# Loops of the weighted sums on TensorE: ten rounds of six instead of six rounds of ten, and a loop in the last two units

## The chip, the core and the metric

The kernel runs on one core of a Trainium2 chip. A core has five engines with queues of their own: TensorE (PE, with the weight loads shown apart as PEld), VectorE (DVE), ScalarE (ACT), GpSimd (POOL) and SyncE (SP), which issues the transfers here; 16 DMA engines carry them out. The metric is the device time of one execution in microseconds, as the median over runs.

## What is computed

Eight sequences decode one token each. An attention with 32 query heads over 16 key and value heads reads the last 2048 positions of its caches (`W = 2048`); beside it stands a layer norm with a two-layer MLP; a sigmoid gate mixes the two results. All tensors are bf16. Cut to what matters:

```python
q = (x @ wq).reshape(B, 1, 32, 128)
scores = einsum(q, k_cache[:, :, Sk - W:]) * 128 ** -0.5
p = softmax(scores)
o = einsum(p, v_cache[:, :, Sk - W:])          # the weighted sum
a = o.reshape(B, 1, 4096) @ wo
h = gelu(layernorm(x) @ w1 + b1)
b = h @ w2 + b2
g = sigmoid((x * gate_w).sum(-1))
out = g * a + (1 - g) * b
```

The two caches make 134 MB of the 154 MB that are read from HBM.

## The kernel before

**Tiling.** The 128 pairs of sequence and key head and the 2048 positions are cut into 16 units (`NU`): 4 groups of two sequences (`NG`), and for each of them 4 parts of 512 positions (`NT`). A unit needs one K transfer and one V transfer of 4096 KB each. The buffer `RAW` has four slots of that size (`ND`); `take_slot` deals them out in the order 1, 2, 0, 3. The list `stream` (L587 to L594) sets the order of the transfers on SP's queue: K0, K1, V0, K2, V1, ..., K15, V14, V15, and then the first 24 parts of w2 ("M 0"), the two halves of wo ("W 0", "W 1") and the last 12 parts of w2 ("M 1", three transfers). A transfer waits until the last reader of its slot is done. For a slot that held V, the last reader is the unit's weighted sum (`slot_free[s] = [pv]`, L789). M 1 takes the slot of V14, and W 0 has a slot of its own.

**One unit.** VectorE transposes K in two halves (L718; in unit 15 in four quarters). TensorE writes a mask to PSUM (L685) and adds the scores to it (L732, the other three of four by the helper line L175). VectorE takes the maximum (L645), ScalarE the exponential with its sum (L646, L649). VectorE transposes the weights (L668) and ScalarE copies them in four parts into their places in `BD` (L674); in unit 15 eight smaller transposes of VectorE do that (L663, four for each half of the sum). Then TensorE forms the weighted sum of V: 64 matmuls of 128 x 256 (`NK // 2`), each with a weight load of its own, all added up in one place of PSUM.

**The weighted sum, where the change is.** `pair(e, n)` (L753 to L756) emits the n-th matmul of a unit with fixed addresses; it shows as L755. In units 0 to 13, `pv_loop` (L758) emits pairs 0 and 1, then a loop of `ROUNDS` = 6 rounds of `RND` = 10 matmuls whose addresses stand in two registers (`reg_matmul`, shown as L188; the registers are advanced at L770, and the branch of the loop is L767), and then pairs 62 and 63. In units 14 and 15 `pv_half` (L782) emits two halves of 32 fixed pairs; the first half of unit 15 can start when half of its weights are in place.

**Order on TensorE.** `_Plan.schedule` sorts all operations by their assumed costs; the lists `pe_hist` keep masks, scores and weighted sums in the order in which they are added: scores of unit t, weighted sum of unit t - 1, mask and scores of unit t + 1. ScalarE's copies (L674) of unit t wait for the weighted sum of unit t - 1 (L891 to L893), since both use `BD`. At the end the order on TensorE is: weighted sum of unit 13, mask and scores of unit 15, first half of unit 14, the group's maximum over its units (L695; L696 on VectorE waits for it), second half of unit 14, first half of unit 15, the group's sum (L703), second half of unit 15, two thirds of M 0's matmuls (L579), the selection matmuls (L819), the last third of M 0, the output projection with W 0 (L579), eight matmuls without a use for their result ("fill", L851 and L175), the projection with W 1, and the three pieces of M 1. Between the second half of unit 15 and the selection matmuls VectorE weights and adds up the four sums of the group (L794 to L808), and behind them it makes `oT` (L822), which both projections need. The last three operations are the copies out of PSUM (L900, L901) and the transfer of the output.

**What a plan's cost changes.** The costs given with an operation (8.8 for a loop, 3.65 for a half) only enter the sorting; the change leaves them as they are.

Of the kernel before, what the change touches and what calls it, by code (L numbers as in the profile page):

```python
# [38 lines left out]
class _Plan:  # L39
# [10 lines left out]
    def add(self, eng, fn, deps=(), name=None, cost=0.1, after=(), prio=0):  # L50
        op = _Op(eng, fn, deps, name, cost, after=after, prio=prio)
        op.idx = len(self.all)
        self.all.append(op)
        return op
# [116 lines left out]
ARENA_BASE = 16512  # L171
# [10 lines left out]
def reg_operand(reg, ap):  # L182
    return mybir.RegisterAccessPattern(ap=ap, dtype=BF, memsetref="arena_set", regref=reg.name, is_regloc_offset=False,
                                       reg_ap_offset=reg.name, const_ap_offset=0, const_sub_tensor_id=0)
# [10 lines left out]
def build_kernel(nc, A_x, A_k_cache, A_v_cache, A_wq, A_wo, B_x, B_w1, B_b1, B_w2, B_b2, gate_w, out):  # L195
    B, Sq, D = A_x.shape
    _, Hkv, Sk, Dh = A_k_cache.shape
# [10 lines left out]
    NK = W // (4 * NT)  # L208
    ND = 4
    SE = 4 * W  # L210
    DE = 2 * SE
# [13 lines left out]
    with ExitStack() as es:  # L225
# [74 lines left out]
        def aoffs(name):  # L300
            return R[name][0] // 2
# [4 lines left out]
        def view(name, parts=128):  # L306
            o, n, dt = R[name]
            a = arena[0:parts, o // 2: o // 2 + (n * (2 if dt == BF else 4)) // 2]
            if dt == F32:
                a = a.bitcast(F32)  # L310
            return a
# [33 lines left out]
        RAW = view("RAW")  # L345
# [6 lines left out]
        def slot(s):  # L352
            return RAW[:, s * DE:min((s + 1) * DE, ND * DE + WOR * D)]
# [8 lines left out]
        def col(i, parts=128):  # L362
# [17 lines left out]
        add, dma = P.add, P.dma  # L380
# [7 lines left out]
                   deps=[o_idf], name="r8", cost=0.2)  # L388
# [210 lines left out]
        qk_hist, pe_hist, dve_ops = [], [], {}  # L599
        qk_unit, qb_done = {}, {}  # L600
        exp_done, sp_done, pv_done, mx_done = {}, {}, {}, {}
# [11 lines left out]
        def load_item(which, nm, t):  # L613
            s = take_slot()
            g, xq = divmod(t, NT)
            k0 = S0 + 4 * NK * xq
            src = ck[which][32 * g:32 * g + 32, k0:k0 + 4 * NK, :].rearrange("i (x r) d -> i x (r d)", x=4)
            d = dma("sp", lambda e: e.dma_start(slot(s), src), "s%d" % s, 8 * W * Dh * 2, deps=slot_free[s], name="%s%d" % (nm, t), after=last_dma[-1:])
            last_dma.append(d)
            slot_free[s] = []  # L620
            return s, d
# [14 lines left out]
        def bd_home(t):  # L636
            return "KT" if t == NU - 1 else "BD"
# [108 lines left out]
        def v_item(t):  # L746
            s, d = load_item(1, "dv", t)
            g, x = divmod(t, NT)
            home = bd_home(t)
            obk, oc = (0, 0) if t == NU - 1 else (BK_OS + x // 2, 256 * (x % 2))  # L750
            dst = ps[:, obk, oc:oc + 256]

            def pair(e, n):  # L753
                q, ee = divmod(n, 2)
                return e.matmul(dst, bass.AP(arena, offset=aoffs(home) + 256 * q + ee, ap=[[AST, 128], [2, 128]]),  # L755
                                slot(s).rearrange("p (r k d) -> p r k d", r=2, d=128)[:, :, n, :], start=(n == 0), stop=(n == NK // 2 - 1), skip_group_check=True)  # L756

            def pv_loop(e):  # L758
                mm = None
                for n in range(2):  # L760
                    pair(e, n)
                if not regs:
                    regs.extend([e.alloc_register("r_p"), e.alloc_register("r_v")])
                rp, rv = regs
                e.reg_mov(rp, ARENA_BASE + 2 * (aoffs(home) + 256 + 254))
                e.reg_mov(rv, ARENA_BASE + 2 * (aoffs("RAW") + s * DE + 256))
                with e.Fori(0, ROUNDS) as _:  # L767
                    for i in range(RND):
                        reg_matmul(nc, e, dst, reg_operand(rp, [[AST, 128], [2, 128]]), reg_operand(rv, [[AST, 128], [DE // 2, 2], [1, 128]]))
                        e.reg_add(rp, rp, 2 if i % 2 == 0 else 510)  # L770
                        e.reg_add(rv, rv, 256)
                for n in range(2 + ROUNDS * RND, NK // 2):
                    mm = pair(e, n)
                return mm

            wait_x = [x_read[g - 1]] if g else [o_u]
            if t < NU - 2:
                pv = add("pe", pv_loop, deps=[d] + sp_done[t][0] + sp_done[t][1] + wait_x, name="pv%d" % t, cost=8.8, after=pe_hist[-1:])
                pe_hist.append(pv)
            else:  # L780
                for v in range(2):
                    def pv_half(e, v=v):  # L782
                        mm = None
                        for n in range(NK // 4 * v, NK // 4 * (v + 1)):
                            mm = pair(e, n)
                        return mm
                    pv = add("pe", pv_half, deps=[d] + sp_done[t][v] + wait_x, name="pv%d_%d" % (t, v), cost=3.65, after=pe_hist[-1:])
                    pe_hist.append(pv)
            slot_free[s] = [pv]  # L789
            src, w = ps[:, obk, oc:oc + 256], k(g, WT + x)  # L790
            if x == 0:
                fn = lambda e, src=src, w=w: e.tensor_scalar(out=X2, in0=src, scalar1=w, scalar2=None, op0=ALU.mult)
            else:
                fn = lambda e, src=src, w=w: e.scalar_tensor_tensor(out=X2, in0=src, scalar=w, in1=X2, op0=ALU.mult, op1=ALU.add)  # L794
            pend.append((fn, "x%d" % t, x))
            pv_of[t] = pv
            if x == NT - 1:
                last = None
                for fn, nm, xx in pend:
                    p = pv_of[t if t < NU - 1 and xx == 2 else NT * g + max(xx, 1)]  # L800
                    last = add("dve", fn, deps=[p, w_done[g], last, xl_done.get(g - 1)], name=nm, cost=0.5, prio=5 if g == NG - 1 else 0, after=dve_ops["sp", t] if xx < NT - 1 else [])
                del pend[:]
                x_read[g] = last
                x0 = add("dve", lambda e: e.tensor_scalar(out=X, in0=X2[:, 0:128], scalar1=maskq[:, 0:1], scalar2=None, op0=ALU.mult), deps=[last, o_maskq], name="xa%d" % g, cost=0.25, prio=6 if g == NG - 1 else 0)
                last = add("dve", lambda e: e.scalar_tensor_tensor(out=X, in0=X2[:, 128:256], scalar=maskq[:, 1:2], in1=X, op0=ALU.mult, op1=ALU.add), deps=[x0], name="xb%d" % g, cost=0.3, prio=6 if g == NG - 1 else 0)

                hi = add("dve", lambda e: e.tensor_copy(XS[:, 0, :], X), deps=[last, oT_done.get(g - 1)], name="xh%d" % g, cost=0.23, prio=6 if g == NG - 1 else 0)
                lo = add("dve", lambda e: e.tensor_tensor(out=XS[:, 1, :], in0=X, in1=XS[:, 0, :], op=ALU.subtract), deps=[hi], name="xl%d" % g, cost=0.3, prio=6 if g == NG - 1 else 0)  # L808

                xl_done[g] = lo  # L810

                def sel_x(e):
                    mm = None
                    for b in range(NB_):
                        for dq in range(4):
                            for v in range(2):
                                args = (ps[:, BK_S, 64 + 32 * b:64 + 32 * b + 32], seld[:, 4 * b + dq, :], XS[:, v, 32 * dq:32 * dq + 32])
                                st, sp = dq == 0 and v == 0, dq == 3 and v == 1
                                mm = e.matmul(*args, start=st, stop=sp, skip_group_check=True) if v == 0 else held_matmul(nc, e, *args, start=st, stop=sp, skip=True)  # L819
                    return mm  # L820
                sx = add("pe", sel_x, deps=[lo] + o_seld + [oT_done.get(g - 1)] + b6_r[-1:], name="sx%d" % g, cost=0.6, prio=3 if g == NG - 1 else 0)
                oT_done[g] = add("dve", lambda e: e.tensor_tensor(out=bass.AP(arena, offset=aoffs("oT") + NB_ * g, ap=[[AST, 128], [1, NB_], [8, WOP]]),  # L822
                                                                  in0=ps[:, BK_S, 64:128].rearrange("p (b j) -> p b j", b=2),
                                                                  in1=bass.AP(arena_f, offset=foffs("rg"), ap=[[AST // 2, 128], [1, NB_], [0, WOP]]), op=ALU.mult),
                                 deps=[sx, rg_done[g]], name="oT%d" % g, cost=0.45, prio=6 if g == NG - 1 else 0)
                b6_r.append(oT_done[g])

        pend, pv_of, xl_done = [], {}, {}
        regs = []
        ROUNDS, RND = 6, 10  # L830

        def wo_chunk(i):
            s = ND if i == 0 else take_slot()
# [123 lines left out]
```

## Time and profile before

The times of three runs are 364.46, 364.51 and 364.79 us: median 364.51. The profiled execution has a span of 363.0 us, from the first to the last instruction.

| | before |
|---|---|
| median of runs | 364.51 us |
| span of the profiled execution | 363.0 us |
| PE busy | 297.9 us (82%) |
| VectorE busy | 231.4 us (64%) |
| ScalarE busy | 168.6 us (46%) |
| HBM read | 154.29 MB, 425 GB/s over the span |
| looped matmuls (L188) | 840, 277 ns each |
| matmuls with fixed addresses (L755) | 184, 272 ns each |
| branches of the loops (L767) | 84 |

How to read it: matmuls are pipelined, and 277 ns is the way of one from its start to its end, while the next one starts much earlier; the pace is read from the starts in the timeline. "PE" rows are matmuls and "PEld" rows the weight loads ahead of them. A row of the timeline has the start in us, the length, the engine, the line and, in brackets, the idle time of the engine before it and what ended it; "issue" means that the engine waited for nothing that the profile shows. Branches and register instructions are not counted as busy. The page's 40 slices cover 9 us each.

### The profile page before, as it was taken

To read this page: it belongs to the slowest core of one execution; us is meant where nothing else is said; L and a number is where in the kernel's file an instruction comes from. 1 tells how busy PE (TensorE), PEld (TensorE's weight loads), DVE (VectorE), ACT (ScalarE), POOL (GpSimd) and SP (SyncE) were. 2 spreads that over 40 slices of the span, in tenths; PEclk is the share of its full clock that TensorE was granted. 3 is DMA by queue.
4 is the path that set the end of the run, shared out by engine and by line. 5 is a ranking of instruction groups with operands and counts; after the bars stand their busy time and mean duration, and the time that the engine had idled before them with its cause. 6 is when DMAs were issued, how large, how long until landed. Compare 5 with 4: busy or idle time off the path is not lost.

```text
span 363.0 us, 4821 instructions
## 1 busy us (share of the span) xinstructions
PE 297.9 (82%) x1954; PEld 125.3 (35%) x1423; DVE 231.4 (64%) x166; ACT 168.6 (46%) x130; POOL 22.9 (6%) x52
## 2 busy tenths in 40 slices
PE   0456366999999979998897979997989698999875
PEld 0111000434252615242433417150615152436742
DVE  0452989576666694929385768566675949295720
ACT  1022106656647463663637373838374554656000
POOL 9032030000010000000100000000000000003000
PEclk9976598999999998999999989999999999999999
DMA  8999999999999999999999999999999999999996
GB/s 347 436 437 406 455 412 455 412 455 412 450 415 451 415 451 413 441 426 441 426 441 426 435 430 437 430 437 428 437 430 437 430 435 430 437 430 433 415 430 257
DMA packets 6102, 154.45 MB, mean 426 GB/s; under 512 B 694, under 2 KB 840, under 8 KB 1228
## 3 DMA queue, kind: packets, MB, share of 16 engines
q1 hardware_dynamic: 6092, 154.30, 98.8%
q8 instruction: 8, 0.13, 0.1%
q14 instruction: 2, 0.02, 0.0%
HBM read 154.29 MB, written 0.01 MB: 425 GB/s over the span
## 4 chain that ended last, share of the span: by engine, by line
DMA 56%; DVE 27%; PE 14%; issue 1%; ACT 1%; SPq 0%; POOL 0%
DMA arena<-in_A_k_cache_dram 47%; DVE arena L718 21%; PE ps L175 6%; DMA arena<-in_B_w_dram 6%; DMA arena<-in_A_x_dram 3%; DVE arena L668 2%; PE ps L188 2%; PE ps L755 2%; PE ps L732 2%; DVE arena L645 1%; PE ps L501 0%; PE ps L579 0%; DVE arena L557 0%; DVE arena L521 0%; ACT arena L536 0%
## 5 line engine op out<-in xcount | busy, mean ns | idle before, releaser
L718 DVE STREAM_TRANSPOSE arena<-arena 128x4096 f32<-128x4096 f32 (+1 forms) x34 | 141.7, 4175 | 21.9 <-DMA arena<-in_A_k_cache_dram 21.9
L674 ACT ACTIVATE arena<-arena 32x2048 bf16<-32x2048 bf16 x60 | 114.5, 1908 | 71.4 <-DVE arena L668 42.9
L175 PE MATMUL ps<-arena 128*128 128x512 bf16 (+3 forms) x531 | 136.1, 402 | 0.0
L188 PE MATMUL ps<-arena 128*128 x840 | 109.5, 277 | 7.3 <-issue 1.2
L188 PEld LDWEIGHTS ps<-arena 128*128 x840 | 81.4, 97 | 34.3 <-issue 19.0
L732 PE MATMUL ps<-arena 128*128 128x512 bf16 x128 | 51.4, 401 | 27.6 <-DVE arena L718 26.1
L645 DVE TENSOR_REDUCE arena<-ps 128x1 f32<-128x2048 f32 x16 | 36.7, 2291 | 53.8 <-PE ps L175 53.8
L732 PEld LDWEIGHTS ps<-arena 128*128 128x128 bf16 x128 | 12.5, 98 | 131.7 <-issue 75.3
L649 ACT ACTIVATE arena<-ps,arena 128x2048 bf16<-128x2048 f32 x16 | 40.7, 2543 | 0.5
L646 ACT ACTIVATE arena<-arena 128x1 f32<-128x1 f32 x16 | 3.2, 203 | 63.5 <-DVE arena L645 63.5
L755 PE MATMUL ps<-arena 128*128 128x256 bf16 x184 | 25.3, 272 | 1.1 <-DVE arena L663 1.1
L755 PEld LDWEIGHTS ps<-arena 128*128 128x128 bf16 x184 | 16.9, 99 | 18.8 <-issue 14.6
L668 DVE STREAM_TRANSPOSE arena<-arena 128x1024 f32<-128x1024 f32 x15 | 18.1, 1205 | 2.9 <-ACT arena L649 2.9
L579 PE MATMUL ps<-arena 128*8 128x288 bf16 (+1 forms) x140 | 9.6, 286 | 4.0 <-DMA arena<-in_A_wo_dram 3.3
L739 POOL MEMSET arena<- 128x4096 f32 x1 | 3.5, 3511 | 148.2 <-PE ps L175 148.2
L685 PE MATMUL ps<-arena 128*128 128x512 bf16 x16 | 6.5, 407 | 6.5 <-ACT arena L649 5.2
L629 POOL COPY arena<-arena 32x64 bf16<-32x64 bf16 x16 | 3.7, 229 | 123.3 <-PE ps L175 122.4
L901 ACT ACTIVATE arena<-ps 8x288 bf16<-8x288 f32 x1 | 0.4, 402 | 19.5 <-PE ps L579 19.5
L422 DVE COPY arena<-arena 8x128 bf16<-8x128 bf16 x2 | 0.5, 228 | 13.9 <-DMA arena<-in_A_x_dram 13.9
L579 PEld LDWEIGHTS ps<-arena 128*8 128x8 bf16 (+1 forms) x140 | 5.8, 86 | 9.9 <-DMA arena<-in_A_wo_dram 3.3
L900 DVE CAST arena<-ps 8x288 bf16<-8x288 f32 x1 | 0.4, 446 | 12.3 <-PE ps L579 12.3
L557 DVE TENSOR_TENSOR arena<-arena 128x1152 f32<-128x1152 f32 x1 | 1.4, 1358 | 9.7 <-ACT arena L555 9.7
(106 smaller groups left out, 94.0 us busy)
## 6 DMA issues: line engine op xcount, KB each, us to landing
arena<-in_A_k_cache_dram SPq DMA_DIRECT2D x16, 4096.0 KB, 28.7
arena<-in_A_v_cache_dram SPq DMA_DIRECT2D x16, 4096.0 KB, 25.5
arena<-in_B_w_dram SPq DMA_DIRECT2D x1, 4608.0 KB, 22.0
arena<-in_A_wo_dram SPq DMA_DIRECT2D x2, 2304.0 KB, 23.8
arena<-in_A_wq_dram SPq DMA_DIRECT2D x1, 4096.0 KB, 12.6
arena<-in_B_w_dram SPq DMA_DIRECT2D x1, 3456.0 KB, 24.1
arena<-in_B_w_dram SPq DMA_DIRECT2D x1, 1152.0 KB, 22.3
arena<-in_B_w_dram SPq DMA_DIRECT2D x1, 576.0 KB, 23.0
```

The source lines that it names most:

```text
L175: return e.add_instruction(mybir.InstMatmult(name=nc.get_next_instruction_name(), engine=mybir.EngineType.PE, ins=[e.lower_ap(rhs), e.lowe ...
L188: return e.add_instruction(mybir.InstMatmult(name=nc.get_next_instruction_name(), engine=mybir.EngineType.PE, ins=[rhs, lhsT], outs=[e.low ...
L579: ins = e.matmul(ps[32 * j:32 * j + 8, BK_ACC, 0:JN], lhsT, rhs[:, JN * j:JN * j + JN], start=False, stop=True, skip_group_check=True, til ...
L629: return e.tensor_copy(dst, src)
L645: mx = add("dve", lambda e: e.tensor_reduce(out=k(g, MX + x), in_=scores, axis=AXL.X, op=ALU.max), deps=[qk_unit[t]], name="mx%d" % t, cos ...
L649: ex = add("act", lambda e: e.activation(out=bass.AP(arena, offset=aoffs("P"), ap=[[AST, 128], [64, 32], [1, 2], [2, 32]]), in_=ps[:, 0:4, ...
L668: pc = add("dve", lambda e: e.transpose(view("PC").bitcast(F32), view("P").bitcast(F32)), deps=[ex] + (sp_done[t - 1][0] if t else [o_acc0 ...
L674: return e.activation(out=bass.AP(arena, offset=32 * a * AST + aoffs(home) + 64 * a, ap=[[AST, 32], [256, 32], [1, 64]]), in_=bass.AP(aren ...
L685: mm = e.matmul(*args, start=True, stop=False, skip_group_check=True) if n == 0 else held_matmul(nc, e, *args, start=True, stop=False, ski ...
L718: return e.transpose(bass.AP(arena_f, offset=foffs(base) + 2048 * h0, ap=[[AST // 2, 128], [1, 2048 * nh]]), bass.AP(arena_f, offset=foffs ...
L732: mm = e.matmul(*args, start=False, stop=True, skip_group_check=True) if rc == 0 else held_matmul(nc, e, *args, stop=True, skip=True)
L755: return e.matmul(dst, bass.AP(arena, offset=aoffs(home) + 256 * q + ee, ap=[[AST, 128], [2, 128]]), slot(s).rearrange("p (r k d) -> p r k ...
```

## The change

`pv_loop` takes the range of its matmuls, the number of rounds and the matmuls in a round. Units 0 to 13 call it with 10 rounds of 6 (2 + 60 + 2 = 64 as before). The halves of units 14 and 15 call it too, with 7 rounds of 4 (2 + 28 + 2 = 32), so that the two registers are set and the loop is entered four more times.

```diff
-            def pv_loop(e):
+            def pv_loop(e, n0, n1, rounds, rnd):
                 mm = None
-                for n in range(2):
+                for n in range(n0, n0 + 2):
                     pair(e, n)
...
-                e.reg_mov(rp, ARENA_BASE + 2 * (aoffs(home) + 256 + 254))
-                e.reg_mov(rv, ARENA_BASE + 2 * (aoffs("RAW") + s * DE + 256))
-                with e.Fori(0, ROUNDS) as _:
-                    for i in range(RND):
+                e.reg_mov(rp, ARENA_BASE + 2 * (aoffs(home) + 128 * n0 + 256 + 254))
+                e.reg_mov(rv, ARENA_BASE + 2 * (aoffs("RAW") + s * DE + 128 * n0 + 256))
+                with e.Fori(0, rounds) as _:
+                    for i in range(rnd):
                         reg_matmul(nc, e, dst, reg_operand(rp, [[AST, 128], [2, 128]]), reg_operand(rv, [[AST, 128], [DE // 2, 2], [1, 128]]))
                         e.reg_add(rp, rp, 2 if i % 2 == 0 else 510)
                         e.reg_add(rv, rv, 256)
-                for n in range(2 + ROUNDS * RND, NK // 2):
+                for n in range(n0 + 2 + rounds * rnd, n1):
                     mm = pair(e, n)
                 return mm
...
-                pv = add("pe", pv_loop, deps=[d] + sp_done[t][0] + sp_done[t][1] + wait_x, name="pv%d" % t, cost=8.8, after=pe_hist[-1:])
+                pv = add("pe", lambda e: pv_loop(e, 0, NK // 2, 10, 6), deps=[d] + sp_done[t][0] + sp_done[t][1] + wait_x, name="pv%d" % t, cost=8.8, after=pe_hist[-1:])
...
-                    def pv_half(e, v=v):
-                        mm = None
-                        for n in range(NK // 4 * v, NK // 4 * (v + 1)):
-                            mm = pair(e, n)
-                        return mm
-                    pv = add("pe", pv_half, deps=[d] + sp_done[t][v] + wait_x, name="pv%d_%d" % (t, v), cost=3.65, after=pe_hist[-1:])
+                    pv = add("pe", lambda e, v=v: pv_loop(e, NK // 4 * v, NK // 4 * (v + 1), 7, 4), deps=[d] + sp_done[t][v] + wait_x, name="pv%d_%d" % (t, v), cost=3.65, after=pe_hist[-1:])
...
-        ROUNDS, RND = 6, 10
```

## The prediction

> **What bounds the kernel now.** I read the page first (busy time, the 40 slices, the DMA queues), then the chain of waits, then the timeline of the last 35 us and of single loops.
>
> ```profile
> span 363.0 us, 4821 instructions
> ...
> DMA  8999999999999999999999999999999999999996
> ...
> q1 hardware_dynamic: 6092, 154.30, 98.8%
> q8 instruction: 8, 0.13, 0.1%
> ```
>
> The 16 DMA engines are busy from the first slice to the last: 154.30 MB at 98.8%. The profiled execution has a span of 363.0 us, and the median of the runs is 364.51 us, so 1.5 us lie around the span; I carry that difference over unchanged. TensorE can only matter in two ways: it frees the buffers that the next transfers need, and it has work left when the last transfer has landed. The chain of waits (start, length, what) shows the second place:
>
> ```profile
> 312.51 0.22 PE ps L755 x2
> 312.73 1.14 PE ps L188 x10
> ...
> 319.80 1.33 PE ps L188 x10
> 321.13 0.36 PE ps L755 x2
> 321.49 0.22 PE ps L685
> ...
> 329.87 3.49 PE ps L755 x32
> 333.37 0.12 PE ps L695 x2
> 333.48 3.53 PE ps L755 x32
> ...
> 337.03 22.31 DMA arena<-in_B_w_dram
> ...
> 359.38 1.71 PE ps L579 x24
> ...
> 361.12 0.45 DVE arena L900
> ```
>
> Three things are to be seen. The weighted sum of unit 13 is a loop (L188) with two unrolled pairs (L755) on each side; from 312.51 to 321.49 it takes 8.98 us for 64 matmuls, 0.140 us each. The unrolled halves of unit 14 take 3.49 us for 32, 0.109 us each: looping is dearer. And the last weight transfer, issued at 337.03 when the second half of unit 14 frees its buffer, needs 22.31 us to land, because other transfers stand ahead of it in the queue; the kernel ends on that landing plus 24 small matmuls and the copy out.
>
> **What a round costs.** The timeline of the weight loads of unit 13 (start, length, engine, line; in brackets the idle time before):
>
> ```profile
> 316.91 1.15 PEld L188 LDWEIGHTS ps<-arena 128*128 x10 [0.33 <-issue]
> 318.35 1.15 PEld L188 LDWEIGHTS ps<-arena 128*128 x10 [0.30 <-issue]
> ```
>
> ```profile
> L767 PEldq COMPARE_BRANCH  x84: 69/201/235, 68.7 to 321.0; - x84
> ```
>
> A round of ten lasts 318.35 - 316.91 = 1.44 us. Inside it ten loads take 1.15 us; the last one itself is about 0.10, so the steps are (1.15 - 0.10) / 9 = 0.117 us. What is left, 1.44 - 1.17 = 0.27 to 0.28, is the round's end: a gap of 0.30 us in which nothing issues. The branch is in it: 84 branches are 14 units times 6 rounds, with a median of 201 ns, and the shortest (69 ns) are those that leave the loop. So I write a round of r matmuls as 0.117 r + b, with **b = 0.28 us** for each taken branch. The trace has rounds of one size only, so that b is the same for six and for four is an assumption. Its bounds: 0.31 (the 0.30 gap with the widest branch in place of the median, 0.235 - 0.201, less rounding) and, if a shorter body made the taken branch as cheap as the one that falls through, 0.28 - (0.201 - 0.069) = 0.15.
>
> [...]
>
> **The change part by part.** *Units 0 to 13, ten rounds of six.* The matmuls are the same 60; taken branches go from 5 to 9 per unit: 4 x 0.28 = +1.1 us of TensorE per unit. It is hidden by the transfers:
>
> ```profile
> DMA to landing us min/median/max: 18.8/25.5/37.3
> ...
> 60.00:134.00 74.00, 69.97 (x418) 28.82 (x299) 53.23 (x28) 45.50 (x33) 0.92 (x4) 1.00 1.00 432
> 134.00:298.00 164.00, 144.57 (x904) 61.97 (x652) 110.36 (x71) 89.11 (x64) 0.92 (x4) 0.98 1.00 432
> ```
>
> The first line is of the V transfers, which wait for a weighted sum to free a buffer; the other two are windows, with PE's busy time after the window's length. A 4 MB transfer takes 4.19 / 0.432 = 9.7 us, so even the V transfer with the shortest way (18.8 us) had 9 us of other transfers ahead of it. Between 60 and 134 us TensorE is nearly full (69.97 of 74) and falls behind by up to 1.1 us a unit, some 4 us over the four units there; that leaves 5 us of queue. Afterwards it has 19.4 us idle in 164 (8.5 units of 19.4 us), or 2.3 us a unit against 1.1, so it catches up before the last units. Without that cover the price would be up to 14 x 1.1 = 15 us; it would be gone only if b were about double. What is late next is unit 13, the last long loop: mask and scores of unit 15 follow it on TensorE, +1.1 us.
>
> *Units 14 and 15, four halves of seven rounds of four.* Per half: 28 looped matmuls at 0.117 in place of 0.109 (+0.2), six taken branches (6 x 0.28 = +1.68), the way out (the two pairs behind the loop above take 0.36 in place of 0.22, +0.14) and the two register loads at its start (below 0.1; I take 0.06): **+2.08 us** on 3.49. These stand one after the other on TensorE, and this is the view of what follows them:
>
> ```profile
> 321.59 7.70 ACT L674 ACTIVATE arena<-arena 32x2048 bf16<-32x2048 bf16 x4 [3.90 <-PE ps L755]
> ...
> 335.08 5.84 DVE L663 STREAM_TRANSPOSE arena<-arena 32x512 f32<-32x512 f32 x8 [1.41 <-ACT arena L649]
> ...
> 338.14 3.65 PE L755 MATMUL ps<-arena 128*128 128x256 bf16 x32 [1.14 <-DVE arena L663]
> ...
> 345.63 0.48 DVE L794 SCALAR_TENSOR_TENSOR arena<-ps,arena 128x256 f32<-128x256 f32 x1 [2.74 <-PE ps L755]
> 345.67 2.13 PE L579 MATMUL ps<-arena 128*8 128x288 bf16 x32
> ...
> 348.23 1.15 PE L579 MATMUL ps<-arena 128*8 128x288 bf16 x16
> 348.33 0.44 DVE L822 TENSOR_TENSOR arena<-ps,arena 128x64 bf16<-128x64 f32 x1 [0.92 <-PE ps L175]
> 351.23 2.13 PE L579 MATMUL ps<-arena 128*8 128x288 bf16 x32 [1.85 <-DMA arena<-in_A_wo_dram]
> 353.29 0.39 PE L851 MATMUL ps<-arena 128*128 128x512 bf16 x1
> 353.51 1.67 PE L175 MATMUL ps<-arena 128*128 128x512 bf16 x7
> 356.65 2.13 PE L579 MATMUL ps<-arena 128*8 128x288 bf16 x32 [1.46 <-DMA arena<-in_A_wo_dram]
> 359.38 1.70 PE L579 MATMUL ps<-arena 128*8 128x288 bf16 x24 [0.61 <-DMA arena<-in_B_w_dram]
> ```
>
> ScalarE's copies for unit 14 (L674) start on the end of unit 13's loop, so they are also 1.1 late, and the first half starts at 330.8. TensorE waits 1.14 us ahead of unit 15 for the transposes (L663); it now comes later than they do, so this wait is eaten. VectorE's minimum (L696) stands ahead of those transposes and waits for a matmul behind the first half: the transposes start about 2 us late, end by 343, and unit 15's halves start at 342.2 and 347.9; the first four of eight are done by 340, so nothing waits. The end of unit 15's sum, and with it L794, moves by
>
> 1.1 + 4 x 2.08 - 1.14 = **8.3 us**.
>
> The weight transfers issued at 337.03 go out at 342.2; of their 22.31 us about 4 are their own 1.7 MB, so 18 us of queue stand ahead and 5 us less do not show. That step costs nothing.
>
> Then the tail. L822, which makes the attention result, ends at 357.1 in place of 348.8; the 16 matmuls ahead of the first output projection end at 357.45, and the projection starts there, not at 351.23 (it waited for a landing, 1.85). It keeps 2.06 us to the filler; the eight filler matmuls take 8 x 0.213 = 1.71 (from 1.67 for seven); the second projection starts at 361.2 in place of 356.65. Its 32 matmuls take 1.90 at (2.13 - 0.29) / 31 = 0.0595 each, the 24 last ones 1.37 to the last start plus 0.29: 364.8 in place of 361.1. The tail had 4.6 us of slack, and **3.7 us** come through: 364.51 + 3.7 = **368.2 us**. In general: shift = 28 b + 0.46, end = 364.5 + (shift - 4.6) where that is positive.
>
> The code gets shorter; all of it is 8 packets and 0.13 MB by the page's row for q8, and a sixth less of that is below 0.1 us of DMA.
>
> **The rivals.** *No change* (the other side): the branch is cheaper in a short body, or TensorE's sequencer runs ahead. One mechanism decides: b. At 0.148 us the shift is 4.6 and everything fits in the waits for landings: 364.5 us. For it speaks that one loop did run at full pace:
>
> ```profile
> 218.82 6.71 PE L188 MATMUL ps<-arena 128*128 x60
> ```
>
> That is 0.109 each, branches hidden. Against it: there TensorE was busy with earlier matmuls for 2 us after the loop could issue; at the end the halves follow each other, and the only wait ahead of one (1.14) is eaten.
>
> *Dearer rounds.* In unit 12 the rounds took 301.77 - 300.03 = 1.74 us, 0.3 more than in unit 13:
>
> ```profile
> 300.03 1.38 PE L188 MATMUL ps<-arena 128*128 x10 [0.37 <-issue]
> 301.77 1.33 PE L188 MATMUL ps<-arena 128*128 x10 [0.36 <-issue]
> ```
>
> The trace does not say why this loop and not others. If it falls on one of the halves: 6 x 0.3 = +1.8, 370.0 us. [...]
>
> *Faster*: only by less instruction traffic, 0.1 us; I see no path to 0.2%.
>
> **How the numbers follow.** A measurement here tells about 0.2% (0.7 us) from no change. Forecast (b from 0.22 to 0.31: 366.5 to 369.1 us): 0.56. Dearer rounds, 369 to 370.2: 0.17. No change, with b at 0.17 or less: 0.23. Faster: 0.03; slower by another way (a starved queue, or a clock that drops in the thinner loops; the windows above, full of loops of ten, were granted 1.00 and 0.98): 0.01. Slower is therefore 0.74, same 0.23, faster 0.03. The range has to take in the no-change case, as it holds more than 0.2: 364.3 to 370.2.
>
> **What would show it.** Right: in unit 13 the weight loads come in groups of six with gaps of 0.30 (0.98 us a round), in units 14 and 15 groups of four at 0.75; a half takes 5.6 us; the wait of 1.14 at L663 is gone; L794's last start is near 353.9; the wait of the projections for in_A_wo_dram and the last for in_B_w_dram are gone and the chain's end is TensorE, from unit 13 on, not the 22.31 us of DMA; DMA stays at 9 in all slices but the last. Wrong: gaps below 0.15 us, or a projection that still waits for its landing.

## The result and the profile after

| | before | after |
|---|---|---|
| median of the runs | 364.49 us | 367.26 us (367.16 to 367.89) |
| ratio, with its 95% interval | | 1.0077 (1.0063 to 1.0092) |
| span of the profiled execution | 363.0 us | 366.4 us |
| last landing of a weight transfer | 360.7 us | 360.6 us |

The change costs 2.8 us. The profiled execution of the changed kernel was the longest of its four (367.89 us), so its span shows 3.4 us, 0.6 more than the medians.

The page of the changed kernel, its first lines and the DMA part:

```profile
span 366.4 us, 5029 instructions
...
DMA  8999999999999999999999999999999999999992
...
q1 hardware_dynamic: 6092, 154.30, 97.8%
q8 instruction: 7, 0.11, 0.1%
```

The DMA engines work through all slices but the last, as before, and move the same 154.30 MB; the share fell from 98.8 to 97.8% because the span got longer at its end. The chain of waits (start, length, what) ends otherwise:

```profile
350.16 0.67 PE ps L188 x4
351.69 0.67 PE ps L188 x4
353.51 2.06 PE ps L579 x32
356.06 3.04 PE ps L579 x48
359.42 1.51 PE ps L175 x7
360.93 3.55 PE ps L579 x56
```

Where 22.31 us of DMA and 24 matmuls stood, there is now TensorE: the short loops (L188), then the matmuls of w2 and the projections (L579) with the filler (L175) between them, without a gap for a landing (only the selection matmuls wait 0.25 us for VectorE, at 355.49). The 48 are the last third of M 0 and the first projection, the 56 the second projection and M 1; before, each of them was split by a wait for a transfer.

The timeline of the weight loads in the first half of unit 15 (start, length; in brackets the idle time before) shows the rounds:

```profile
342.36 0.47 PEld L188 LDWEIGHTS ps<-arena 128*128 x4
343.13 0.44 PEld L188 LDWEIGHTS ps<-arena 128*128 x4 [0.31 <-issue]
343.90 0.44 PEld L188 LDWEIGHTS ps<-arena 128*128 x4 [0.33 <-issue]
344.64 0.48 PEld L188 LDWEIGHTS ps<-arena 128*128 x4 [0.31 <-issue]
```

Four loads, a gap of 0.31 us, four loads: (344.64 - 342.36) / 3 = 0.76 us a round, where the prediction had 0.75. The branch itself, over 14 x 10 + 4 x 7 = 168 of them:

```profile
L767 PEldq COMPARE_BRANCH  x168: 72/208/238, 68.6 to 353.0; - x168
```

Its median is 208 ns (201 before) with bodies of six and four. VectorE's timeline gives the two points between which the tail lies, the last weighting step of the sum (L789, which was L794) and the copy out (L894, which was L900):

```profile
336.89 0.16 DVE L696 TENSOR_REDUCE arena<-ps 128x1 f32<-128x2 f32 x1 [3.08 <-PE ps L695]
336.97 5.84 DVE L663 STREAM_TRANSPOSE arena<-arena 32x512 f32<-32x512 f32 x8
...
353.55 0.48 DVE L789 SCALAR_TENSOR_TENSOR arena<-ps,arena 128x256 f32<-128x256 f32 x1 [4.67 <-PE ps L755]
...
364.50 0.45 DVE L894 CAST arena<-ps 8x288 bf16<-8x288 f32 x1 [7.96 <-PE ps L579]
```

The sum's end moved from 345.63 to 353.55, by **7.9 us**; the copy out from 361.12 to 364.50, by **3.4 us**. So the tail took up 4.5 us. The transposes (L663) start 1.9 us late behind L696, and nothing waits for them.

### The profile page after: what moved, and what is told of

The parts are those of the page before. It is cut to its first block, busy times and chain, and to the rows that moved or that the text cites. A ratio compares the mean times of both kernels' runs of the same rounds, so it can differ in the third digit from the quotient of the medians.

```text
span 366.4 us, 5029 instructions
## 1 busy us (share of the span) xinstructions
PE 309.6 (84%) x1954; PEld 124.6 (34%) x1423; DVE 231.6 (63%) x166; ACT 168.7 (46%) x130; POOL 23.0 (6%) x52
## 3 DMA queue, kind: packets, MB, share of 16 engines
q1 hardware_dynamic: 6092, 154.30, 97.8%
## 4 chain that ended last, share of the span: by engine, by line
PE 50%; DMA 26%; DVE 18%; issue 4%; ACT 1%; SPq 0%; POOL 0%
DMA arena<-in_A_k_cache_dram 23%; PE ps L188 23%; PE ps L175 16%; DVE arena L718 13%; PE ps L732 5%; DMA arena<-in_A_x_dram 3%; PE ps L579 2%; PE ps L755 2%; DVE arena L668 1%; DVE arena L645 1%; PE ps L685 1%; PE ps L501 0%; DVE arena L557 0%; DVE arena L521 0%; ACT arena L536 0%
## 5 line engine op out<-in xcount | busy, mean ns | idle before, releaser
L188 PE MATMUL ps<-arena 128*128 x952 | 136.4, 278 | 16.4 <-issue 2.6
L175 PE MATMUL ps<-arena 128*128 128x512 bf16 (+3 forms) x531 | 134.9, 401 | 0.0
L188 PEld LDWEIGHTS ps<-arena 128*128 x952 | 92.1, 97 | 59.5 <-issue 42.5
L732 PE MATMUL ps<-arena 128*128 128x512 bf16 x128 | 50.6, 395 | 15.4 <-DVE arena L718 13.2
L732 PEld LDWEIGHTS ps<-arena 128*128 128x128 bf16 x128 | 12.5, 98 | 118.9 <-issue 81.6
L755 PE MATMUL ps<-arena 128*128 128x256 bf16 x72 | 13.6, 273 | 0.0
L685 PE MATMUL ps<-arena 128*128 128x512 bf16 x16 | 6.5, 407 | 6.5 <-ACT arena L649 5.2
L755 PEld LDWEIGHTS ps<-arena 128*128 128x128 bf16 x72 | 5.5, 100 | 17.1 <-issue 15.6
L579 PE MATMUL ps<-arena 128*8 128x288 bf16 (+1 forms) x140 | 9.5, 290 | 0.0
L789 DVE SCALAR_TENSOR_TENSOR arena<-ps,arena 128x256 f32<-128x256 f32 x12 | 5.7, 478 | 4.7 <-PE ps L755 4.7
L579 PEld LDWEIGHTS ps<-arena 128*8 128x8 bf16 (+1 forms) x140 | 5.9, 86 | 5.3 <-issue 3.2
## 6 DMA issues: line engine op xcount, KB each, us to landing
arena<-in_A_v_cache_dram SPq DMA_DIRECT2D x16, 4096.0 KB, 23.5
```

The lines of the kernel that those rows point to most:

```text
L175: return e.add_instruction(mybir.InstMatmult(name=nc.get_next_instruction_name(), engine=mybir.EngineType.PE, ins=[e.lower_ap(rhs), e.lowe ...
L188: return e.add_instruction(mybir.InstMatmult(name=nc.get_next_instruction_name(), engine=mybir.EngineType.PE, ins=[rhs, lhsT], outs=[e.low ...
L579: ins = e.matmul(ps[32 * j:32 * j + 8, BK_ACC, 0:JN], lhsT, rhs[:, JN * j:JN * j + JN], start=False, stop=True, skip_group_check=True, til ...
L685: mm = e.matmul(*args, start=True, stop=False, skip_group_check=True) if n == 0 else held_matmul(nc, e, *args, start=True, stop=False, ski ...
L732: mm = e.matmul(*args, start=False, stop=True, skip_group_check=True) if rc == 0 else held_matmul(nc, e, *args, stop=True, skip=True)
```

## The experiments

All edits are to the changed kernel, and each is cut to the call of the weighted sum that it replaces: `pv_loop(e, 0, NK // 2, 10, 6)` for units 0 to 13 and `pv_loop(e, ..., 7, 4)` for a half of unit 14 or 15. "Unrolled" below stands for the fixed pairs of the kernel before.

**Units 0 to 13 alone** (e1_main_only):

```diff
-  lambda e, v=v: pv_loop(e, NK // 4 * v, NK // 4 * (v + 1), 7, 4)
+  lambda e, v=v: [pair(e, n) for n in range(NK // 4 * v, NK // 4 * (v + 1))][-1]
```

> Ten rounds of six in units 0 to 13, the last two units unrolled as before. Theory (the loss is TensorE's late chain behind the last two units): unit 13's loop ends 1.1 us later, the wait of 1.14 us ahead of unit 15's first half takes it up, the last L794 step starts within 0.3 us of 345.6, and the time is that of before, 364.5 us (within 0.2%). Rival (slower loops in units 0 to 13 free the V slots later and the transfers lose time): the whole loss, about +2.8 us, is here.

Measured: 364.53 us, ratio 0.9998 (0.9989 to 1.0007). The time is that of before, and the rival is out. One detail of the expectation was wrong, as VectorE's timeline shows:

```profile
336.57 5.84 DVE L663 STREAM_TRANSPOSE arena<-arena 32x512 f32<-32x512 f32 x8 [1.41 <-ACT arena L649]
...
347.12 0.48 DVE L789 SCALAR_TENSOR_TENSOR arena<-ps,arena 128x256 f32<-128x256 f32 x1 [2.74 <-PE ps L755]
```

Both are 1.5 us later than before (335.08 and 345.63). The wait ahead of unit 15 does not take up unit 13's delay, because the transposes it waits for hang on the same late scores; it is only eaten when the halves of unit 14 get longer. The tail hid the 1.5 us.

**The halves alone** (e2_ends_only):

```diff
-  lambda e: pv_loop(e, 0, NK // 2, 10, 6)
+  lambda e: pv_loop(e, 0, NK // 2, 6, 10)
```

> Six rounds of ten in units 0 to 13 as before, seven rounds of four in the halves of units 14 and 15. Theory: four halves at +2.0 to 2.1 us less the eaten wait of 1.14 us move the end of unit 15's sum by 7.0 us, of which the tail takes up about 4.5: +2.4 us in the profiled execution, +1.8 to +2.5 in the times. Rival (the loss comes from units 0 to 13): no change, 364.5 us.

Measured: 366.29 us, ratio 1.0047 (1.0033 to 1.0061): +1.7 us, just under the range expected; the sum's end moved to 351.99 (+6.4, not 7.0) and the copy out to 362.94 (+1.8). The halves carry the loss; unit 13's 1.1 us adds to them only because the tail is already used up.

**The same loops with one taken branch** (e3_ends_2x14) **and with thirteen** (e4_ends_14x2), in place of six:

```diff
-  pv_loop(e, NK // 4 * v, NK // 4 * (v + 1), 7, 4)
+  pv_loop(e, NK // 4 * v, NK // 4 * (v + 1), 2, 14)     # e3
+  pv_loop(e, NK // 4 * v, NK // 4 * (v + 1), 14, 2)     # e4
```

> The changed kernel with the halves in two rounds of fourteen in place of seven of four: one taken branch for each half, and the same entries, register loads and looped matmuls. Theory (the cost is 0.28 us for each taken branch): a half costs +0.7 us, the end of the sum moves by 2.8 us, the tail hides it, 364.5 us. Rival (the cost is entering and leaving a loop, or matmuls with addresses in registers): as slow as the change, +2.8 us.

> The changed kernel with the halves in fourteen rounds of two: thirteen taken branches for each half in place of six. Theory: a half costs 0.2 + 13 x 0.28 + 0.2 = +4.0 us over the unrolled one, the end of the sum moves by 16 us, 4.5 of them hidden: +11.7 us, 376 us. If a shorter body made the branch cheaper (0.15 us): a half costs +2.4, +5 us, 369.5 us.

Measured: 364.53 us for two rounds, ratio 1.0003 (0.9994 to 1.0012), and 375.64 us for fourteen, ratio 1.03 (1.0284 to 1.0316). Looping, registers and entry are there in both, so the taken branch is the price. VectorE's timeline of the kernel with two rounds and then of the one with fourteen:

```profile
347.86 0.48 DVE L789 SCALAR_TENSOR_TENSOR arena<-ps,arena 128x256 f32<-128x256 f32 x1 [3.16 <-PE ps L755]
...
361.14 0.45 DVE L894 CAST arena<-ps 8x288 bf16<-8x288 f32 x1 [10.29 <-PE ps L579]
```

```profile
361.69 0.48 DVE L789 SCALAR_TENSOR_TENSOR arena<-ps,arena 128x256 f32<-128x256 f32 x1 [6.59 <-PE ps L755]
...
372.65 0.45 DVE L894 CAST arena<-ps 8x288 bf16<-8x288 f32 x1 [7.95 <-PE ps L579]
```

The weight loads of the latter, two in a round, have the same gap as six or four:

```profile
340.54 0.21 PEld L188 LDWEIGHTS ps<-arena 128*128 x2 [0.31 <-issue]
341.06 0.21 PEld L188 LDWEIGHTS ps<-arena 128*128 x2 [0.30 <-issue]
```

Put side by side (starts in the timelines; the chain is the time from the first matmul of unit 14's sum to the last weighting step; in the kernel before, 1.14 us of it are the wait ahead of unit 15, so 15.92 - 1.14 = 14.78 us are work):

| | taken branches per half | first matmul, unit 14 | last weighting step | chain | per half over before | copy out | copy out less weighting |
|---|---|---|---|---|---|---|---|
| before | none | 329.71 | 345.63 | 15.92 | | 361.12 | 15.49 |
| e3 | 1 | 330.98 | 347.86 | 16.88 | +0.53 | 361.14 | 13.28 |
| changed | 6 | 330.87 | 353.55 | 22.68 | +1.98 | 364.50 | 10.95 |
| e2 | 6 | 329.78 | 351.99 | 22.21 | +1.86 | 362.94 | 10.95 |
| e4 | 13 | 331.10 | 361.69 | 30.59 | +3.95 | 372.65 | 10.96 |

One to six branches add 0.29 us each, six to thirteen 0.28; with e2's 1.86 in the middle it is 0.27 and 0.30. Each row is a single execution, so the firm figure is the one over the whole stretch, from one to thirteen: 0.285 us. The kernel before has one more short wait, ahead of the group's sum:

```profile
341.69 0.30 PEld L703 LDWEIGHTS ps<-arena 128*128 128x128 f32 x2 [0.19 <-ACT arena L702]
```

By the starts of the matmuls around it, it holds up the chain by 0.17 us. The table leaves it in the work; taken off, it would raise each figure per half by 0.04.

The last column shows where the tail stops hiding: it shrinks from 15.49 to 10.95 us and no further, which is the work there without a wait for a landing. The slack is 15.49 - 10.95 = 4.54 us, and beyond it every microsecond came through in the three kernels that pass it (10.95, 10.95 and 10.96 us).

**Unit 14 alone looped** (e8_unit14_only):

```diff
-  lambda e, v=v: pv_loop(e, NK // 4 * v, NK // 4 * (v + 1), 7, 4)
+  lambda e, v=v: pv_loop(e, NK // 4 * v, NK // 4 * (v + 1), 7, 4) if t == NU - 2 else [pair(e, n) for n in range(NK // 4 * v, NK // 4 * (v + 1))][-1]
```

> The changed kernel with unit 15's halves unrolled: two looped halves in place of four. Theory (shift less slack): 1.1 + 2 x 2.05 - 1.14 = 4.1 us of shift, less than the 4.5 us of the tail, so no change against before, 364.5 us. Rival (each looped half costs its share): half of the loss, +1.4 us.

Measured: 364.57 us, ratio 1.0002 (0.9993 to 1.0011). The last weighting step starts at 349.46, 3.8 us late, and the time does not move. Two looped halves are free, four cost 2.8 us: a threshold, not a share.

**Without the filler** (e5_no_fill):

```diff
-                filler("fill", 8, o_m2[-1:])
+                pass
```

> The changed kernel without the eight filler matmuls between the two output projections. Theory (in the changed kernel TensorE's own work ends last from unit 15 on): the eight times 0.213 us come off, -1.7 us against the changed kernel, about 365.6 us, +1.0 against before. Rival (the end still hangs on the landings): no change against the changed kernel. Rival (the clock drops without the filler): slower than the changed kernel.

Measured: 365.48 us, ratio 1.0026 (1.0017 to 1.0036) to before; 1.8 us less than the changed kernel. The filler is part of what ends last in the changed kernel. The clock row of its page shows 9 (90% or more) in all the last slices, and its mean granted clock was 0.967 (0.963 in the changed kernel), so the rival with the clock falls. Up to the filler this kernel is the changed one, so its trace is a second one of the halves:

```profile
352.95 0.48 DVE L789 SCALAR_TENSOR_TENSOR arena<-ps,arena 128x256 f32<-128x256 f32 x1 [4.54 <-PE ps L755]
...
361.98 0.45 DVE L894 CAST arena<-ps 8x288 bf16<-8x288 f32 x1 [6.03 <-PE ps L579]
```

Here the sum ends 7.32 us later than before, not 7.92. Its first matmul of unit 14 starts at 330.94, so the chain is 22.01 us and a half costs 1.81 us over before.

**The cover over units 0 to 13 taken away** (e7_main_15x4, halves unrolled):

```diff
-  lambda e: pv_loop(e, 0, NK // 2, 10, 6)
+  lambda e: pv_loop(e, 0, NK // 2, 15, 4)
```

> Fifteen rounds of four in units 0 to 13 (14 taken branches in place of 5), the last two units unrolled as before. Theory: +2.5 us per unit makes a unit on TensorE 19.8 to 20 us, more than the 19.4 us of its two transfers; TensorE becomes the bound from unit 0 on, unit 13 starts some 16 us late, and the end moves by +11 to +15 us: 376 to 380 us. Rival (the cover over units 0 to 13 holds at any pace, or is a queue 9 us deep that refills): 364.5 us.

Measured: 379.10 us, ratio 1.0395 (1.0379 to 1.0411). The V transfers tell how near the changed kernel is to this. From issue to landing, and DMA share and GB/s at the end of the window's row, first of the changed kernel and then of this one:

```profile
134.00:298.00 164.00, 151.00 (x923) 61.89 (x656) 114.35 (x74) 92.58 (x66) 0.92 (x4) 1.00 1.00 433
...
DMA to landing us min/median/max: 17.1/23.5/36.9
```

```profile
134.00:298.00 164.00, 148.43 (x849) 59.00 (x624) 107.36 (x65) 85.12 (x63) 0.92 (x4) 1.00 0.98 413
...
DMA to landing us min/median/max: 13.6/14.8/36.9
```

With 9 more branches a unit the median way of a V transfer falls from 25.5 us (before) to 14.8, of which 9.7 are its own, and the rate from 432 to 413 GB/s: as far as these figures tell, buffers come free too late. The 4 more branches of the change cost 2 us of that queue (23.5) and, by e1, nothing in time.

**No loop at all** (e6_all_unrolled), **units 0 to 4 unrolled** (e9_unroll_5) **and units 0 to 8** (e10_unroll_9):

```diff
-  lambda e: pv_loop(e, 0, NK // 2, 10, 6)
+  lambda e: [pair(e, n) for n in range(NK // 2)][-1]                                   # e6
+  lambda e: [pair(e, n) for n in range(NK // 2)][-1] if t < 5 else pv_loop(e, 0, NK // 2, 6, 10)   # e9; 9 in e10
```

with the halves unrolled in all three.

> No loops at all: all 16 units in fixed pairs, some three times the instructions on TensorE's queue. Theory (the transfers bound the kernel once TensorE's last chain fits into the tail): 364.5 us as before, within 0.2%, plus at most 0.5 us for the instruction transfers (0.1 to 0.2 MB more at 430 GB/s). Rival (loops are there because code loading stalls TensorE): slower than before by more than 0.2%.

Measured: 365.91 us, ratio 1.0037 (1.0023 to 1.0051). Not as expected: without a taken branch on TensorE the kernel is 1.4 us slower than before. Its page and its chain:

```profile
q1 hardware_dynamic: 6092, 154.30, 98.4%
q8 instruction: 13, 0.21, 0.2%
```

```profile
338.87 22.33 DMA arena<-in_B_w_dram
...
361.25 1.75 PE ps L579 x24
...
363.02 0.45 DVE arena L894
```

The end hangs on the landings again, and these are late: 361.20 in place of 359.34 for the first of the three last pieces. They are issued at 338.87, 1.8 us later than before, but e8 issues them at 342.32 and loses nothing. The granted clock is lower too, 0.930 to 0.939 against 0.953 to 0.972 of the kernel before, but the profiled execution of e10 below, at 0.977, takes 365.62 us all the same.

The trace has 16 landings for such a transfer; by their number, one for each of the 16 DMA engines. For the last piece, with the number of instruction packets, 16 KB each by the rows of q8 (0.13 MB in 8, 0.21 MB in 13):

```
                 packets   earliest 8 landings   next landings        latest
before              8        359.03 to 359.96    8 to 360.74
changed             7        358.97 to 359.56    8 to 360.62
no loop            13        359.41 to 360.43    3 to 361.09          5 from 362.06 to 362.64
```

With eight packets, eight landings are about 1 us behind the others; with 13, 13 - 8 = 5 are later again by as much. (The seventh packet of the changed kernel starts only at 358.8; six of its landings are at 360.47 or later.) In the trace of the kernel without loops a packet takes 0.88 to 0.96 us, which is about the size of the step. That made the step theory, which the other two runs test:

> The kernel before with units 0 to 4 unrolled, and the other loops as they were: some 450 instructions more on TensorE's queue, so 9 or 10 instruction packets of 16 KB in place of 8 (13 without any loop, where the last landings came 1.9 us late). Step theory (the packets go round eight of the 16 DMA engines, each delays its engine's share of every later transfer by about 1.5 us, and the last engine sets the landing): the ninth packet meets an engine that has had one, so the whole loss of 1.4 us is here if that packet comes before the last transfers: 365.9 us, and the landings of the last transfer show one or two engines late. Proportional theory (0.28 us for each packet over eight): 364.8 to 365.1 us. No-link theory: 364.5 us.

> The same with units 0 to 8 unrolled: 11 or 12 packets. Step theory: 365.9 us as with 13 packets, with three or four engines late. Proportional theory: 365.3 to 365.6 us. No-link theory: 364.5 us.

Measured: 365.88 us with 10 packets, ratio 1.0035 (1.0022 to 1.0049), and 365.87 us with 11, ratio 1.0036 (1.0023 to 1.0050). With 10 packets two landings of the last piece are at 362.3 and 362.5 and the rest by 361.05; with 11 packets three are from 361.99 to 362.10 and the rest by 360.59. The loss is the same with 10, 11 and 13 packets, and the number of late landings is that of the packets over eight. It also grows within a run: of W 0, which lands some 10 us earlier, four landings are late without loops (12 packets by then), one in e9 (9 packets) and two in e10 (10 packets). The transfers take 98.8% of the 16 DMA engines' span before and 98.4% without loops; the three kernels with two to five packets over eight were 1.4 us slower than before, which has eight.

## Why the prediction was right, step by step

- **The price of a taken branch, 0.28 us, the same for short bodies.** Right: 0.285 from one to thirteen branches a half; with the 1.98, 1.86 (e2) or 1.81 (e5) of six branches in between, the two stretches give 0.26 to 0.31. The gap is mostly 0.30 to 0.31 us with bodies of ten, six, four and two. The rival of a cheaper branch (0.15 us, no change) falls: a compare-and-branch took 201 to 208 ns in the median, and the gap around it 0.3 us.
- **+2.08 us per half.** Too much, and this is the term that was mis-sized: 1.98 on the mean in the profiled execution of the changed kernel, 1.86 in e2 and 1.81 in e5. The share that does not grow with the branches was 0.53 - 0.28 = 0.25 us, where the prediction had 0.40 for leaving, entering and the slower pace. The prediction also left out that the first round's end of a second half, behind the two small matmuls of the group (L695, L703), can be shorter. The weight loads of the changed kernel's second half of unit 14 show a first gap of 0.16 in place of 0.31; in e5 both second halves start with two rounds without a gap, but in e2 the one behind L703 has 0.28. No run shows why.

```profile
336.82 0.42 PEld L188 LDWEIGHTS ps<-arena 128*128 x4
337.41 0.44 PEld L188 LDWEIGHTS ps<-arena 128*128 x4 [0.16 <-issue]
338.16 0.53 PEld L188 LDWEIGHTS ps<-arena 128*128 x4 [0.31 <-issue]
```

- **The shift of the sum's end, 8.3 us.** 7.9 measured in the profiled execution, 7.3 in e5. Unit 13 gave 1.16 (330.87 against 329.71), the eaten wait of 1.14 is gone from the timeline, and so is the short one at L703, which the prediction did not count.
- **Slack of 4.6 us in the tail.** 4.54, the same in three kernels; the work behind it, 10.95 us, was worked out right (364.8 - 353.9 = 10.9).
- **+3.7 us.** 3.4 in the profiled execution, by the 0.4 of the shift; 2.8 in the medians. e5 shows where the other 0.6 can lie: with its halves the shift is 7.32 us, and 7.32 - 4.54 = 2.8. In the profiled execution of the changed kernel, the longest of its four, the same rounds took a little longer; why one execution has them longer stays open.
- **The range, 364.3 to 370.2 us.** It took in no change as well, so the time alone would say little for the mechanism. The signs named in advance do: rounds of six at 1.00 us (0.98 predicted), rounds of four at 0.76, no wait of TensorE left for L663 or for a landing, and a chain that ends on TensorE.
- **Units 0 to 13 cost nothing.** Right (e1: ratio 0.9998). The cover has the end that was seen: with nine more branches a unit, 2.5 us in place of 1.1, it was gone (e7, +14.6 us).
- **The weight transfers issued 5 us late cost nothing.** Right: issued at 342.4, the last landed at 360.6.
- **Dearer rounds** of 0.3 us more did not come: the rounds of the halves start at most 0.84 us apart, most of them 0.74 to 0.81; in e5 it is at most 0.80.
- **Fewer instructions, below 0.1 us.** Right for this change, and for the wrong reason. The 16 KB of a packet would be 0.04 us at the 432 GB/s of all engines together; one packet took 0.88 to 1.02 us in the traces of before and of the changed kernel. The counts of late landings read as if each packet delayed one engine, and with seven packets the last landing stayed where it was with eight (360.62 and 360.74 us).

None of the kernels beat the one before. Three equal it: the change with the halves unrolled (e1), with the halves in two rounds (e3), and with unit 14 alone looped (e8).

## What to carry to other kernels

The loops on TensorE were priced here by their taken branches (0.285 us each, with bodies of fourteen, four and two), not by their length: read the gap between two rounds in the weight loads (0.30 to 0.31 us here, mostly), and multiply. In this kernel, which its transfers bound, the price was free until it passed the slack of the place where it stood, so work out two slacks, that of the queue in the middle and that of the last chain behind the last landing (4.54 us): the loops of units 0 to 13 were free (e1, ratio 0.9998), and with those of the last two units the cost was 2.8 us. Unrolling was not free either: without loops there were 13 instruction packets in place of 8, and the time was 1.4 us longer. So count the packets, and look in the landings of the last transfers for some that fall behind the others.

## What was not expected of the hardware

The landings fit instruction packets that go round eight of the 16 DMA engines, and two packets over eight cost as much as five (365.88, 365.87 and 365.91 us with 10, 11 and 13 packets, 364.51 before, with 8; nine were not run). That it is the packets themselves that hold these engines up is inferred from the counts of late landings (2, 3 and 5); no row names the engine that carried a packet.
